# Blockwise causal attention with a gated output layer: ten transposes of the attention output go from TensorE to transposing transfers, in a new order of work

## Chip, cores and metric

One core of one Trainium2 chip runs the kernel; the seven others are idle. The metric is the device time of one execution in microseconds (us), the median of the runs given. Lower is better.

## What is computed

Two layers in a row. First attention over 8 batches and 8 heads, 576 positions of 64 features each, under a mask of blocks of 64 positions: a position sees all positions of its own block and of the blocks before it. Then a gated linear unit over the 512 features that the 8 heads make together: a causal convolution of 5 taps gives the gate, a matrix product gives the value, and their product goes through an output matrix.

```python
def _attn_ref(q, k, v):                       # [8, 8, 576, 64] each
    scores = (1.0 / np.sqrt(D)) * np.matmul(q, k.transpose(0, 1, 3, 2))
    mask = (pos[:, None] // 64) >= (pos[None, :] // 64)
    scores = np.where(mask, scores, -1000000000.0)
    attn = np.exp(scores - np.max(scores, axis=-1, keepdims=True))
    attn = attn / (np.sum(attn, axis=-1, keepdims=True) + 1e-09)
    return np.matmul(attn, v)

def _moe_ref(x, w_val, conv_w, w_out):        # x: [8, 576, 512]
    for k in range(5):
        gate_pre += conv_w[k] * xp[:, k:k + S, :]     # xp: x behind 4 rows of zeros
    gate = 1.0 / (1.0 + np.exp(-gate_pre))
    return (gate * (x @ w_val)) @ w_out
```

## The kernel before, in words

**Pieces of work.** Each batch has 4 pairs of heads, so there are 32 pairs `p` (batch `p // 4`) and 16 quads `Q` of four heads (two pairs, `2Q` and `2Q + 1`; half a batch). A quad's q and k are loaded (`Lq`, `Lk`, lines 159 to 168), cast to 16 bits (`cq`, `ck`) and turned feature-major by VectorE's stream transposes (`dq`, `dk`, line 202). TensorE makes the scores in three thirds `s.Q.0` to `s.Q.2` (line 236); ScalarE takes the exponentials `e.p.t` of one pair and third (line 244); GpSimd writes zeros over the masked corners (`m.p`, line 261). The last 64 rows of a batch have a small piece of their own (`sl.b`, `el.b`). `av.p` (line 270) multiplies by V on TensorE, with a column of ones beside V that gives the sum; `n.p` (line 286) divides by that sum on VectorE, a reciprocal and a product, and writes the pair's output `x16` in 16 bits, position-major, into one of 4 buffers.

**From position-major to feature-major.** The second layer needs features on the partitions. `xtr.p` (line 294) transposes the 128-position blocks of pairs `p` and `p + 1`, five each, on TensorE: ten transposes into two PSUM banks. `xt.p` (line 302) copies the two banks into the batch's `xts` tile in SBUF, which has room for 4 pairs of 4 + 576 + 64 columns; there are two such tiles, used by batches in turn. `xe.b` (line 305) copies the last 64 columns, with the 4 before them, to the tile of the tails.

**Second layer.** Of each batch, "token groups" `n` = 0 to 7 hold the first 512 positions and `n` = 8, 9 hold the tails of four batches each. `cn.n` (line 321) is the convolution on TensorE, 80 small matmuls with diagonal weights that read `xts` at five offsets; `th.n.s` (line 331) its tanh on ScalarE; `val.n.x` (line 336) the value's matmuls, which also read `xts`; `gv.n.x` (line 345) joins gate and value on VectorE; `o.n.t` (line 352) multiplies by the output matrix; `oc.n.t` (line 360) copies the result out of PSUM on VectorE or ScalarE; `st.n.t` (line 369) stores it.

**Order.** Nothing here is chosen by a scheduler. The string `PLAN` (line 11) lists the steps in one order, and each engine runs its own steps in the order of that list. A word is a step and, behind the `@`, its engine (`A` ScalarE, `D` VectorE, `P` GpSimd, `S` SyncE) or its PSUM banks (digits, two banks for each digit where the step takes a pair). The loop at line 450 issues them. Waits on data and on buffers come from the framework. All transfers but two go through SyncE's queue (SP), where one that waits keeps all behind it back.

Of the kernel before, what the change touches and what calls it, by code (L numbers as in the profile page):

```python
# [20 lines left out]
e.4.1@A xt.2.2@D xe.0@P wv.2@P ck.4@P wv.3@D Lv.1.3@S e.5.1@A cn.0@04 m.5@P dk.3@D dq.3@D Lv.1.2@S
Lv.1.1@S th.0.0@A val.0.0@2 cv.1.2@P gv.0.0@D Lvt.1@S val.0.1@3 th.0.1@A Lq.4@S s.3.2@06 Lwo.0@S
val.0.3@2 e.7.2@A gv.0.1@D sl.1@46 dk.4@D gv.0.3@D Lq.5@S cv.1.1@P e.6.2@A cv.1.3@D Lwo.3@S
val.0.2@3 Lvt.2@S gv.0.2@D el.1.0@A cq.4@D px.1@P pp.5@P s.3.0@04 cvt.1@P el.1.1@A e.6.0@A e.7.0@A
Lwo.1@S dq.4@D cv.1.0@P av.5@6 s.3.1@20 n.5@D m.4@P av.4@4 Lv.2.0@S cq.5@D e.7.1@A Lk.5@S e.6.1@A
m.7@P n.4@D m.6@P s.4.0@06 av.7@2 av.6@4 e.8.0@A ck.5@P n.7@D n.6@D e.9.0@A Lk.6@S s.4.1@06 e.8.1@A
# [14 lines left out]
e.17.0@A n.14@D n.15@D o.2.1@0 oc.2.1@D Lv.5.2@S s.8.2@26 Lk.10@S e.16.2@A xtr.14.2@4 xtr.12.2@0
Lk.11@S xt.14.2@D e.17.2@A cq.10@P o.2.0@2 oc.2.0@A s.8.1@46 xt.12.2@D e.16.1@A e.17.1@A cn.3@02
cq.9@P cv.4.3@D val.3.1@4 val.3.2@5 Lvt.5@S dk.9@D xe.3@P Lv.5.1@S dq.9@D th.3.0@A gv.3.1@D th.3.1@A
s.9.0@06 e.18.0@A gv.3.2@D val.3.0@4 gv.3.0@D cvt.5@D e.19.0@A o.2.2@5 Lq.11@S oc.2.2@D sl.4@02
cv.4.0@P dq.10@D o.2.3@4 el.4.0@A cvt.4@P cv.4.1@P Lv.6.3@S s.9.1@06 el.4.1@A e.18.1@A oc.2.3@D
m.16@P Lk.12@S cv.4.2@P st.1.1@S e.19.1@A ck.10@D av.16@2 n.16@D cn.8@40 val.8.0@6 th.8.1@A th.8.0@A
m.17@P s.9.2@02 e.19.2@A dk.10@D gv.8.0@D val.3.3@7 ck.12@P gv.3.3@D av.17@4 e.18.2@A Lv.5.0@S
s.10.0@26 n.17@D cq.11@A Lv.6.1@S m.19@P e.20.0@A av.19@0 st.2.0@S m.18@P av.18@4 val.8.1@2 e.21.0@A
n.19@D n.18@D s.10.1@06 e.20.1@A xtr.16.2@4 gv.8.1@D Lq.12@S e.21.1@A xtr.18.2@2 xt.16.2@D xt.18.2@D
s.10.2@04 e.20.2@A ck.11@P e.21.2@A cn.4@26 m.21@P cq.12@P dq.11@D th.4.0@A dk.11@D xe.4@P o.3.1@0  # L50
oc.3.1@D val.4.0@1 th.4.1@A s.11.0@24 m.20@P gv.4.0@D val.4.3@0 o.3.0@1 cv.5.3@A e.23.0@A cv.5.2@P
cv.5.1@D gv.4.3@D sl.5@46 e.22.0@A val.4.1@0 el.5.0@A el.5.1@A s.11.1@24 cv.5.0@D val.4.2@6 Lvt.6@S
dq.12@D oc.3.0@A gv.4.1@D gv.4.2@D e.22.1@A o.3.3@7 Lk.14@S dk.12@D ck.14@P st.2.1@S e.23.1@A
oc.3.3@A Lk.13@S s.11.2@02 av.20@4 e.22.2@A Lk.15@S n.20@D av.21@6 o.4.0@0 e.23.2@A oc.4.0@A
s.12.0@24 e.24.0@A e.25.0@A n.21@D xtr.20.2@6 Lv.7.3@S Lq.13@S Lv.6.0@S m.22@P cq.13@A xt.20.2@D
m.23@P av.23@0 st.3.0@S av.22@2 n.23@D s.12.1@46 e.25.1@A Lv.7.1@S o.3.2@0 n.22@D oc.3.2@D
xtr.22.2@2 xt.22.2@D Lv.6.2@S ck.13@P e.24.1@A cv.6.3@D o.4.1@1 cv.6.1@A Lv.7.0@S oc.4.1@A Lq.14@S
s.12.2@46 cn.5@20 dk.13@D xe.5@P e.25.2@A m.25@P dq.13@D e.24.2@A o.4.3@6 oc.4.3@D o.4.2@7 cv.6.0@D
th.5.1@A th.5.0@A oc.4.2@D sl.6@04 el.6.1@A o.8.1@6 Lv.7.2@S el.6.0@A s.13.2@02 Lq.15@S Lvt.7@S
cvt.7@D val.5.0@7 dk.14@D cq.14@P oc.8.1@D e.27.2@A dq.14@D e.26.2@A val.5.1@4 gv.5.0@D s.13.0@25  # L60
e.27.0@A val.5.3@0 e.26.0@A gv.5.1@D val.5.2@1 s.13.1@46 cq.15@P st.3.1@S e.27.1@A e.26.1@A cvt.6@D
o.8.0@2 m.24@P cv.6.2@D gv.5.3@D gv.5.2@D o.5.0@3 ck.15@D m.26@P cv.7.1@P s.14.0@06 oc.8.0@A
oc.5.0@A av.25@4 e.29.0@A av.26@2 dq.15@D dk.15@D e.28.0@A av.24@6 n.25@D s.14.1@04 e.29.1@A m.27@P
# [6 lines left out]
o.6.0@4 o.6.3@5 xt.30.2@A oc.6.3@A cn.7@26 oc.6.1@A th.7.1@A xe.7@P th.7.0@A oc.6.2@D val.7.1@0  # L70
gv.7.1@D val.9.0@1 val.7.3@5 cn.9@26 th.9.0@A gv.9.0@D val.9.1@0 th.9.1@A val.7.2@2 gv.9.1@D
oc.6.0@A val.7.0@1 gv.7.2@D o.9.0@0 o.9.1@4 gv.7.0@D st.6.1@S gv.7.3@D oc.9.1@A st.6.0@S o.7.0@1
oc.9.0@D o.7.1@0 o.7.2@2 oc.7.0@A o.7.3@1 oc.7.1@D st.9.0@S st.7.0@S oc.7.2@D oc.7.3@AD st.7.1@SA
# [411 lines left out]
```

## Time and profile before

| | |
|---|---|
| median of 3 runs | 176.98 us (176.69 to 178.0) |
| the profiled execution | 176.23 us |
| its span, from first to last instruction | 174.4 us, so 1.8 us lie around it |
| mean granted TensorE clock | 0.971 |
| busy: TensorE matmul (PE) | 161.7 us, 93% |
| busy: TensorE weight load (PEld) | 94.8 us, 54% |
| busy: VectorE (DVE) | 129.9 us, 74% |
| busy: ScalarE (ACT) | 131.5 us, 75% |
| busy: GpSimd (POOL) | 69.2 us, 40% |
| moved by DMA | 40.30 MB, 231 GB/s over the span |

A line of a group gives the source line, the engine and its operation, what is written and read, the shape and the count; then the busy time and the mean length of one; then how long the engine was idle before these instructions and what ended that. A line of the timeline starts with the start and the length in us and ends with a count. The matmuls of the profile overlap, so what a step costs TensorE is read from its start to the next step's start, not from its length.

### The profile page before, as it was taken

The numbers are of one execution on the slowest core, as the hardware profiler recorded it, in microseconds if no ns is written. First come the engines' busy times: TensorE is split into PE (matmuls) and PEld (weight loads), VectorE is DVE, ScalarE is ACT, GpSimd is POOL, SyncE is SP. The second block draws the span as 40 slices with busy tenths as digits, with TensorE's granted clock in tenths as the row PEclk, the third lists the DMA queues.
The fourth block names the chain that finished last, engine by engine and source line by source line (L and its number), as shares of the span: only waits on it lengthen the run. The fifth ranks groups of instructions, "written<-read, shape, count | busy, mean of one in ns | idle before, by whom it ended". The sixth has DMA issues, their size and how long they took to land.

```text
span 174.4 us, 6916 instructions
## 1 busy us (share of the span) xinstructions
PE 161.7 (93%) x3013; PEld 94.8 (54%) x3013; DVE 129.9 (74%) x202; ACT 131.5 (75%) x160; POOL 69.2 (40%) x141
## 2 busy tenths in 40 slices
PE   7448999989999999999999999999999999999990
PEld 2123677367445673576366854675437563855640
DVE  1599399998878887879697798779899836741650
ACT  3039999987969899767979799899879698456320
POOL 1284565954595817085505134433603022210000
PEclk9985599999999999999999999999999999999999
DMA  5999997999799699999997596999320005403246
GB/s 176 397 323 296 381 327 195 312 264 301 194 336 271 187 325 334 277 296 319 343 337 242 114 402 198 305 233 357 136 79 2 4 4 194 172 4 120 81 163 241
DMA packets 48216, 40.30 MB, mean 231 GB/s; under 512 B 38453, under 2 KB 38453, under 8 KB 48186
## 3 DMA queue, kind: packets, MB, share of 16 engines
q1 hardware_dynamic: 47898, 39.01, 72.8%
q10 hardware_dynamic: 288, 0.85, 1.4%
q8 instruction: 23, 0.38, 0.9%
q14 instruction: 7, 0.06, 0.1%
HBM read 30.42 MB, written 9.44 MB: 228 GB/s over the span
## 4 chain that ended last, share of the span: by engine, by line
PE 70%; DVE 12%; ACT 7%; issue 5%; DMA 3%; ACTq 0%; DVEq 0%
PE PS L99 65%; ACT pt L242 6%; PE PS L298 5%; DMA qks<-in_q_dram 3%; DVE x L290 3%; DVE qk L156 2%; DVE kT L202 2%; DVE gv L347 2%; DVE qT L202 1%; DVE osb L156 1%; DVE rc L289 1%; ACT osb L156 1%; DVE xt L156 0%; DVE v16t L156 0%; ACT v L156 0%
## 5 line engine op out<-in xcount | busy, mean ns | idle before, releaser
L242 ACT ACTIVATE pt<-PS 128x1024 f16<-128x1024 f32 (+1 forms) x112 | 97.8, 937 | 23.3 <-PE PS L99 20.9
L99 PE MATMUL PS<-qT,kT 32*128 32x64 f16 (+4 forms) x768 | 37.6, 291 | 5.7 <-DVE kT L202 4.5
L99 PEld LDWEIGHTS <-pt 128*128 128x128 f16 x960 | 32.0, 99 | 7.1 <-issue 3.1
L99 PE MATMUL PS<-w_out,gv 128*128 128x512 f16 x144 | 35.3, 380 | 0.1
L347 DVE SCALAR_TENSOR_TENSOR gv<-th,PS 128x512 f16<-128x512 f32 x36 | 24.0, 681 | 14.6 <-ACT th L332 9.3
L156 POOL CAST qk<-qks 128x1152 f16<-128x1152 f32 x22 | 25.3, 1165 | 21.4 <-DVE kT L202 12.3
L99 PE MATMUL PS<-v,pt 128*128 128x65 f16 x896 | 33.0, 195 | 0.9 <-ACT pt L242 0.7
L99 PE MATMUL PS<-xt,w_val 128*128 128x512 f16 x128 | 31.9, 381 | 0.0
L99 PEld LDWEIGHTS <-kT 32*128 32x128 f16 x768 | 16.2, 95 | 28.2 <-issue 16.7
L263 POOL MEMSET pt<- 64x384 f16 x32 | 13.8, 430 | 37.8 <-ACT pt L242 37.1
L290 DVE TENSOR_TENSOR x<-PS,rc 128x640 f16<-128x640 f32 x32 | 26.4, 824 | 1.1
L99 PEld LDWEIGHTS <-w_val 128*128 128x128 f16 x160 | 13.7, 98 | 14.6 <-issue 3.8
L99 PEld LDWEIGHTS <-gv 128*128 128x128 f16 x144 | 12.8, 98 | 14.4 <-issue 0.9
L202 DVE STREAM_TRANSPOSE qT<-qk 128x576 f32<-128x576 f32 x16 | 19.9, 1243 | 0.1
L202 DVE STREAM_TRANSPOSE kT<-qk 128x576 f32<-128x576 f32 x16 | 19.7, 1243 | 0.0
L332 ACT ACTIVATE th<-PS 128x1024 f32<-128x1024 f32 (+1 forms) x20 | 17.7, 947 | 2.2 <-PE PS L99 2.2
L156 DVE COPY osb<-PS 128x512 f32<-128x512 f32 (+1 forms) x20 | 13.4, 671 | 7.3 <-PE PS L99 5.8
L156 ACT COPY osb<-PS 128x512 f32<-128x512 f32 (+1 forms) x17 | 9.7, 583 | 9.0 <-PE PS L99 8.3
L289 DVE RECIPROCAL rc<-PS 128x10 f32<-128x10 f32 x32 | 6.8, 212 | 8.4 <-PE PS L99 5.7
L156 DVE COPY xt<-PS 128x1152 f16<-128x1152 f16 x14 | 10.2, 754 | 3.8 <-PE PS L298 3.7
L156 POOL COPY xtl<-xt 128x272 f16<-128x272 f16 x7 | 3.9, 551 | 22.0 <-DVE xt L156 16.7
L156 POOL CAST v<-vst 128x512 f16<-128x512 f32 x18 | 11.4, 642 | 3.0 <-DMA vst<-in_v_dram 2.4
(45 smaller groups left out, 113.8 us busy)
## 6 DMA issues: line engine op xcount, KB each, us to landing
qks<-in_q_dram SPq DMA_DIRECT2D x16, 576.0 KB, 7.0
qks<-in_k_dram SPq DMA_DIRECT2D x15, 576.0 KB, 7.0
vst<-in_v_dram SPq DMA_DIRECT2D x32, 256.0 KB, 6.4
out_dram<-osb SPq DMA_DIRECT2D x15, 512.0 KB, 4.3
out_dram<-osb SPq DMA_DIRECT2D x5, 256.0 KB, 2.5
vtst<-in_v_dram SPq DMA_DIRECT2D x8, 128.0 KB, 5.4
th<-in_moe_w_val_dram SPq DMA_DIRECT2D x2, 512.0 KB, 8.9
w_st<-in_moe_w_out_dram SPq DMA_DIRECT2D x4, 256.0 KB, 8.7
```

The lines of the kernel that those rows point to most:

```text
L99: nc.tensor.matmul(out=out, lhsT=lhsT, rhs=rhs, start=start, stop=stop, skip_group_check=True)
L156: (eng.copy if eng is nc.scalar else eng.tensor_copy)(out=o, in_=i)
L202: m.transpose(out=o.bitcast(fp32)[..., 0], in_=qk16[(2 * Q + i) % NQ16][0:128].bitcast(fp32))
L242: nc.scalar.activation(out=o, in_=i, func=AF.Exp, bias=0.0, scale=0.125)
L263: m.memset(pt[64:128, 0:2, 0:1536].rearrange("p h (t s) -> p h t s", t=3)[:, :, :, 0:64], 0.0)
L289: nc.vector.reciprocal(out=rc, in_=O[:, :, :, 64:65])
L290: nc.vector.tensor_tensor(out=x16[p % NX16][0:128].rearrange("p i h d -> p h i d"), in0=O[:, :, :, 0:64], in1=rc.to_broadcast([128, 2, 5, ...
L298: nc.tensor.transpose(out=f16(bk(m, e))[:, 128 * i:128 * i + 128], in_=x16[(p + e) % NX16][0:128, i, 0:2, 0:64], identity=ident16[0:128, 0 ...
L332: nc.scalar.activation(out=ths[turn(n) % NTH][0:128, 2 * s:2 * s + 2, 0:width(n)], in_=two(slot["cn", n][s])[:, :, 0:width(n)], func=AF.Ta ...
L347: nc.vector.scalar_tensor_tensor(out=gvs[turn(n) % NGV][0:128, e * x:e * x + e, 0:w], in0=ths[turn(n) % NTH][0:128, e * x:e * x + e, 0:w], ...
```

## The change

- `xtr` and `xt` of pairs 20, 22, 24, 26 and 28 (quads 10 to 14, batches 5 and 6 and half of batch 7) are gone: 50 TensorE transposes, four copies on VectorE and one on ScalarE.
- In their place stand ten steps `xd.p`, p = 20 to 29, on SyncE's queue: each is one transposing transfer of one pair, from `x16` (128 positions by 5 x 128) straight into `xts` (128 features by 5 x 128). Quads 0 to 9 and quad 15 stay on TensorE.
- `xts` is laid out 16 + 576 + 64 columns wide instead of 4 + 576 + 64, and the readers are shifted by 12 columns.
- The order of the list is kept up to the scores of quad 7 (`s.7.0`), with other PSUM banks in places, and is a new one from there to the end. In the new one some steps change engine (`xt.12` and `ck.14` go to ScalarE, `xt.30` to VectorE, some casts and copies likewise), and the last copy of the program, `oc.7.3`, is one instruction on ScalarE and no longer two halves on ScalarE and VectorE.

```diff
-    xts = ring(NX, [128, 4, 644], fp16, "xt")
+    xts = ring(NX, [128, 4, 656], fp16, "xt")
...
     def evac_x(p, cnt, m):
-        copy(m, xts[(p // 4) % NX][0:128, p % 4:p % 4 + 2, 4:580], f16(two(slot["xtr", p]))[:, :, 0:576])
+        copy(m, xts[(p // 4) % NX][0:128, p % 4:p % 4 + 2, 16:592], f16(two(slot["xtr", p]))[:, :, 0:576])
+
+    def dma_x(p, m):
+        m.dma_start_transpose(out=xts[(p // 4) % NX][0:128, p % 4, 16:656].rearrange("p (i s) -> p i s", s=128),
+                              in_=x16[p % NX16][0:128].rearrange("p i h d -> p (i h d)"))
...
-        copy(m, xtl[b // 4][0:128, 0:4, pr, 0:68, o], xts[b % NX][0:128, 0:4, 512:580])
+        copy(m, xtl[b // 4][0:128, 0:4, pr, 0:68, o], xts[b % NX][0:128, 0:4, 524:592])
...
-            return xts[n % NX][r, g, kk:kk + 512]
+            return xts[n % NX][r, g, 12 + kk:524 + kk]
...
-        m.memset(xts[i][0:128, 0:4, 0:4], 0.0)
+        m.memset(xts[i][0:128, 0:4, 12:16], 0.0)
...
-        "xe": ends_x, "cn": conv, "th": gate, "val": val, "gv": gated, "o": proj, "oc": evac_out, "st": store, "cwc": cast_taps, "cw": taps,
+        "xe": ends_x, "xd": dma_x, "cn": conv, "th": gate, "val": val, "gv": gated, "o": proj, "oc": evac_out, "st": store, "cwc": cast_taps, "cw": taps,
```

Of the list itself, the stretch that turns batch 6 (quads 12 and 13) and holds its convolution `cn.6`, with what stood there before:

```diff
-o.5.3@0 cv.7.3@D s.15.1@24 xtr.26.2@6 xt.26.2@D oc.5.3@A e.30.1@A xtr.24.2@0 s.14.2@26 xt.24.2@D
-xe.6@P e.31.1@A e.29.2@A m.29@P cn.6@04 o.5.2@6 e.28.2@A val.6.0@7 m.28@P cv.7.0@P th.6.0@A oc.5.2@D
...
+cvt.7@P av.27@2 s.14.1@04 cv.7.0@P e.28.1@A n.24@D n.27@D o.5.2@6 oc.5.2@D e.29.1@A s.15.1@20
+e.30.1@A o.5.3@7 xd.26@S o.5.1@6 e.31.1@A xd.24@S oc.5.1@A xd.27@S s.14.2@24 oc.5.3@D e.29.2@A
+Lv.7.2@S cn.6@06 m.29@P val.6.3@4 e.28.2@A m.28@P val.6.1@5 th.6.1@A cv.7.1@D gv.6.3@D th.6.0@A
```

**TensorE ahead of `cn.6`.** `qT`, `kT` are the turned queries and keys of one quad, `x` the pairs' outputs (buffers 0 to 3), `DG` the diagonal weights of the convolution. Before:

```order
L99 MATMUL PS<-qT_92,kT_95 128x64
...
L298 MATMUL PS<-ident_63,x_2_115 128x128
...
L298 MATMUL PS<-ident_63,x_1_114 128x128
...
L99 MATMUL PS<-qT_94,kT_97 128x320
...
L99 MATMUL PS<-xt_117,DG 32x512
```

Now:

```order
L99 MATMUL PS<-qT_92,kT_95 128x64
...
L99 MATMUL PS<-w_out,gv_123 128x512
...
L99 MATMUL PS<-qT_94,kT_97 128x320
...
L99 MATMUL PS<-xt_117,DG 32x512
```

The twenty transposes between `s.15.1` and `s.14.2` are gone, and two output products (`o.5.3`, `o.5.1`) stand there instead; `cn.6` still follows `s.14.2`.

**SyncE's queue around the transfers of batch 5.** `vst` are the staging buffers of V, `osb` those of the output. Now:

```order
L161 DMA qks_76<-in_q_dram 128x1152
L306 DMA_TRANSPOSE xt_118<-x_0_113 128x5x128
L306 DMA_TRANSPOSE xt_118<-x_1_114 128x5x128
L306 DMA_TRANSPOSE xt_118<-x_3_116 128x5x128
L306 DMA_TRANSPOSE xt_118<-x_2_115 128x5x128
L171 DMA vst_85<-in_v_dram 128x8x64
L176 DMA vtst_87<-in_v_dram 64x8x64
L171 DMA vst_78<-in_v_dram 128x8x64
L171 DMA vst_82<-in_v_dram 128x8x64
```

Before, the last loads stood in a row:

```order
L171 DMA vst_82<-in_v_dram 128x8x64
L161 DMA qks_76<-in_q_dram 128x1152
L171 DMA vst_84<-in_v_dram 128x8x64
L161 DMA qks_72<-in_q_dram 128x1152
L176 DMA vtst_87<-in_v_dram 64x8x64
L378 DMA out_dram<-osb_129 128x2x512
```

The transposing transfers of batch 5 stand behind the last load of q; four loads of V (`Lv.7.3`, `Lvt.7`, `Lv.6.0`, `Lv.7.0`) now stand behind them. Those of batch 6 have one load of V behind them (`Lv.7.2`), those of pairs 28 and 29 stores alone.

**VectorE around batch 6.** `rc` and `x` are the two halves of `n`. Before:

```order
L156 COPY osb_129<-PS 128x512
L289 RECIPROCAL rc_110<-PS 128x10
L290 TENSOR_TENSOR x_3_116<-PS,rc_110 128x2x5x64
L156 CAST v_1_99<-vst_85 128x8x64
L156 COPY xt_117<-PS 128x2x576 x2
L156 COPY osb_126<-PS 128x512
```

Now:

```order
L289 RECIPROCAL rc_110<-PS 128x10
L290 TENSOR_TENSOR x_3_116<-PS,rc_110 128x2x5x64
L156 COPY osb_126<-PS 128x512 x2
L156 CAST v_1_99<-vst_83 128x8x64
L351 SCALAR_TENSOR_TENSOR gv_124<-th_122,PS 128x512
```

The two copies of `xt` behind the norms are gone; nothing of VectorE's lies between a norm and the convolution's data any more.

More of the change, by code (lines that the diff above doesn't have):

```diff
@@ L21 @@
[L21 to L26, printed above, removed]
@@ L29 @@
+m.7@P n.4@D m.6@P s.4.0@60 av.7@4 av.6@2 e.8.0@A ck.5@P n.7@D n.6@D e.9.0@A Lk.6@S s.4.1@06 e.8.1@A
+Lwo.2@S Lv.2.2@S wo.1@P xtr.4.2@4 Lv.2.3@S Lq.6@S xt.4.2@D wo.0@P e.9.1@A xtr.6.2@2 s.4.2@04 e.8.2@A
+xt.6.2@D e.9.2@A m.9@P dq.5@D Lv.2.1@S cn.1@26 val.1.0@0 th.1.0@A dk.5@D xe.1@P gv.1.0@D Lq.7@S
 ck.6@P val.1.1@1 s.5.0@24 cq.6@P th.1.1@A e.11.0@A e.10.0@A gv.1.1@D o.0.1@0 oc.0.1@D o.0.2@1
@@ L41 @@
[L41 to L63, printed above, removed]
@@ L70 @@
[L70 to L73, printed above, removed]
+m.13@P th.2.0@A o.1.3@2 oc.1.3@D m.12@P dq.8@D o.1.0@3 sl.3@06 val.2.2@2 th.2.1@A el.3.1@A gv.2.2@D
+ck.8@P s.7.0@46 el.3.0@A cv.3.1@A cv.3.2@D e.15.0@A oc.1.0@A o.1.2@0 Lq.9@S oc.1.2@D val.2.3@1
@@ new lines @@
+Lq.10@S e.14.0@A Lk.9@S s.7.2@26 Lv.4.1@S dk.8@D e.15.2@A Lv.4.0@S val.2.1@0 gv.2.3@D av.12@4
+gv.2.1@D e.14.2@A s.7.1@60 e.15.1@A val.2.0@2 n.12@D Lvt.4@S cq.9@P gv.2.0@D av.13@4 e.14.1@A
+cv.4.1@A s.8.0@02 m.15@P o.2.0@6 n.13@D e.17.0@A av.15@4 m.14@P oc.2.0@D e.16.0@A s.8.2@26 e.16.2@A
+Lk.10@S av.14@0 n.15@D o.2.1@4 ck.9@P n.14@D e.17.2@A oc.2.1@A xtr.12.2@2 xt.12.2@A xtr.14.2@0
+s.8.1@46 xt.14.2@D dk.9@D e.16.1@A cn.3@02 dq.9@D e.17.1@A th.3.1@A Lv.4.2@S cv.4.2@D st.0.1@S
+cvt.4@P val.3.2@4 m.16@P m.17@P th.3.0@A val.3.1@5 s.9.0@26 Lv.4.3@S Lv.5.3@S o.2.3@0 cv.4.0@A
@@ new lines @@
+cv.7.3@P gv.6.0@D s.15.2@02 e.31.2@A m.31@P e.30.2@A m.30@P av.29@6 av.28@4 n.29@D n.28@D av.31@2
+av.30@0 o.6.2@4 n.31@D o.6.0@5 oc.6.2@A st.8.0@S n.30@D xtr.30.2@0 xd.29@S o.6.3@4 xt.30.2@D o.6.1@2
+xd.28@S oc.6.0@D oc.6.3@A cn.7@06 val.7.0@3 th.7.0@A st.5.0@S xe.7@D oc.6.1@D th.7.1@A val.9.0@2
+st.6.0@S cn.9@04 th.9.1@A gv.7.0@D th.9.0@A gv.9.0@D val.7.1@3 val.9.1@4 gv.9.1@D val.7.2@5 gv.7.2@D
+val.7.3@2 o.9.0@4 o.9.1@5 gv.7.3@D gv.7.1@D o.7.0@0 o.7.1@1 o.7.3@2 o.7.2@3 oc.9.1@A oc.7.0@A
+oc.9.0@D oc.7.1@D st.6.1@S st.9.0@S oc.7.2@A st.7.0@S oc.7.3@A st.7.1@SA
```

47 lines of the change are left out of this document (31 added, 16 removed).

## Prediction

> **What bounds the kernel now.** I read the page's busy times first, then a table of windows, then TensorE's timeline.
>
> ```profile
> span 174.4 us, 6916 instructions
> PE 161.7 (93%) x3013; PEld 94.8 (54%) x3013; DVE 129.9 (74%) x202; ACT 131.5 (75%) x160; POOL 69.2 (40%) x141
> ```
>
> The windows give, after the length, the busy time of PE, PEld, DVE, ACT and POOL, the granted clock, the DMA share and GB/s. The first shown begins where the new order does (`s.7.0`).
>
> ```profile
> 67.60:97.00 29.40, 29.38 (x615) 17.84 (x615) 23.36 (x38) 24.09 (x30) 13.18 (x24) 1.00 0.97 294
> 97.00:117.00 20.00, 19.93 (x394) 12.18 (x390) 16.32 (x25) 17.68 (x22) 6.84 (x13) 1.00 0.88 263
> 117.00:142.00 25.00, 24.86 (x438) 13.94 (x431) 22.47 (x34) 21.18 (x28) 5.87 (x12) 1.00 0.32 109
> 142.00:170.20 28.20, 28.15 (x496) 16.26 (x495) 14.08 (x24) 15.64 (x19) 3.83 (x11) 1.00 0.31 115
> ```
>
> In none of these windows is TensorE idle for more than 0.14 us, and its clock is full: it alone is the bound from 67.6 us to the last matmul, and a step taken from it is worth its whole time. VectorE (22.5 of 25.0) and ScalarE (21.2) come close between 117 and 142. The DMA share falls from 0.97 to 0.32: late in the kernel there is room for transfers.
>
> **The steps removed.** The five `xtr` that go, as a group of the stretch 113.5 to 153.3 us (busy us, mean ns of one):
>
> ```profile
> L298 PE MATMUL PS<-ident,x 128*128 128x128 f16 x50 | 3.5, 219 | 0.0
> ```
>
> Matmuls overlap, so what a step costs is read in TensorE's timeline from its start to the next step's start:
>
> ```profile
> 114.01 0.73 PE L298 MATMUL PS<-ident,x 128*128 128x128 f16 x10
> 114.58 0.90 PE L99 MATMUL PS<-v,pt 128*128 128x65 f16 x24
> ...
> 139.76 1.29 PE L298 MATMUL PS<-ident,x 128*128 128x128 f16 x20
> 141.00 0.96 PE L99 MATMUL PS<-qT,kT 32*128 32x320 f16 x16
> 142.00 1.35 PE L99 MATMUL PS<-xt,DG 32*32 32x512 f16 x80
> ...
> 147.51 0.63 PE L99 MATMUL PS<-qT,kT 32*128 32x320 f16 x16
> 148.07 0.91 PE L99 MATMUL PS<-v,pt 128*128 128x65 f16 x24
> ...
> 149.00 0.89 PE L99 MATMUL PS<-v,pt 128*128 128x65 f16 x24
> ...
> 164.81 5.34 PE L99 MATMUL PS<-w_out,gv 128*128 128x512 f16 x24
> ```
>
> `xtr.20` is 114.58 - 114.01 = 0.57, `xtr.26` and `xtr.24` together are 141.00 - 139.76 = 1.24, and `xtr.22` and `xtr.28`, the same ten transposes each, I count like the first: 0.57 + 1.24 + 2 x 0.57 = **2.95 us**, below the group's 3.5, as it must be.
>
> A small wait behind them goes too. `s.14.2` takes 142.00 - 141.00 = 1.00, where the same third of quad 15 takes 148.07 - 147.51 = 0.56: half of its banks were those of `xtr.26` and not yet copied out by `xt`. That is **0.44 us**.
>
> **The copies removed.** Four of VectorE's `xt`, 0.75 us each by the groups below, and one of ScalarE's. Neither engine is the bound, so I count nothing; `xt.12`, moved to ScalarE, costs nothing while `cn.3` waits for `xt.14` on VectorE anyway. If VectorE were the bound, they would be worth 3.0 us more; if `cn.3` had no other wait, `xt.12` would cost the 0.4 us by which ScalarE is the slower.
>
> ```profile
> L347 DVE SCALAR_TENSOR_TENSOR gv<-th,PS 128x512 f16<-128x512 f32 x36 | 24.0, 681 | 14.6 <-ACT th L332 9.3 <-PE PS L99 2.9 <-ACT pt L242 2.1
> ...
> L202 DVE STREAM_TRANSPOSE kT<-qk 128x576 f32<-128x576 f32 x16 | 19.7, 1243 | 0.0
> ...
> L156 DVE COPY xt<-PS 128x1152 f16<-128x1152 f16 x14 | 10.2, 754 | 3.8 <-PE PS L298 3.7
> ...
> L156 ACT COPY osb<-PS 128x512 f32<-128x512 f32 x16 | 9.3, 596 | 6.9 <-PE PS L99 6.2 <-ACT pt L242 0.6
> ...
> L156 ACT COPY xt<-PS 128x1152 f16<-128x1152 f16 x2 | 2.2, 1120 | 3.5 <-PE PS L298 3.5
> ```
>
> **The transfers added.** TensorE no longer turns the data itself; it waits for it at `cn.5`, `cn.6` and `cn.7`. What matters is the last transfer of each batch: from the end of its `av`, through the norm, to the convolution. The norm first:
>
> ```profile
> 138.35 0.82 DVE L290 TENSOR_TENSOR x<-PS,rc 128x640 f16<-128x640 f32 x1
> 139.09 0.42 DVE L156 CAST v<-vst 128x512 f16<-128x512 f32 x1
> ...
> 149.27 0.22 DVE L289 RECIPROCAL rc<-PS 128x10 f32<-128x10 f32 x1 [0.83 <-ACT pt L242]
> 149.53 0.82 DVE L290 TENSOR_TENSOR x<-PS,rc 128x640 f16<-128x640 f32 x1
> ```
>
> `av.28` begins at 148.07 and gives way on TensorE at 149.00; its norm ends at 149.53 + 0.82 = 150.35, 1.35 us later. The work that TensorE has in between, in the new order, from the rows above (a third of scores 0.56; an `o` 5.34 / 6 = 0.89; an `av` 149.00 - 148.07 = 0.93):
>
> - `cn.5`: behind `av.22` stand `s.12.1`, `o.4.3`, `o.3.2`, `s.12.2`, `o.4.1`, `o.4.2`: 2 x 0.56 + 4 x 0.89 = 4.7, less 1.35 leaves **3.3 us**.
> - `cn.6`: behind `av.27` stand `s.14.1`, `o.5.2`, `s.15.1`, `o.5.3`, `o.5.1`, `s.14.2`: 3 x 0.56 + 3 x 0.89 = 4.35, which leaves **3.0 us**.
> - `cn.7`: behind `av.28` stand `av.31`, `av.30`, four `o` and `xtr.30`: 2 x 0.93 + 4 x 0.89 + 0.57 = 6.0, which leaves **4.6 us**.
>
> So the transfers cost TensorE nothing if the last of them takes up to 3 us from the end of its norm to its landing. The trace of before has no transposing transfer; the nearest rows are (KB, median us to landing):
>
> ```profile
> vst<-in_v_dram SPq DMA_DIRECT2D x32, 256.0 KB, 6.4
> out_dram<-osb SPq DMA_DIRECT2D x15, 512.0 KB, 4.3
> out_dram<-osb SPq DMA_DIRECT2D x5, 256.0 KB, 2.5
> ```
>
> One `xd` moves 128 x 640 x 2 bytes = 160 KB, less than any of them. The 6.4 belongs to loads of V that queue at a DMA share near 1; stores of 256 KB, most of them late on idle engines, land in 2.5. At the 294 GB/s of the first window 160 KB are 0.56 us of moving, less than the 1 us at which the norms deliver them. Bounds: **2.5 below, 6.4 above**. I take 2.5, the row that it is nearest to: from 117 us on the engines are two thirds idle, and the list puts the last loads of q and k ahead. That is **0 us** of stall. With 4.3 the stalls are 1.0 + 1.3 + 0 = 2.3 us; with 6.4 they are 3.1 + 3.4 + 1.8 = 8.3 us.
>
> SP stands at each `xd` until its norm is done, and four loads of V queue behind those of batch 5. The first to be needed, `Lv.6.0`, is used by `av.25`, and ahead of that TensorE has the rest of the 3.3 us, `cn.5` (1.3 like the row at 142.00), four `val` of batch 5 (four matmuls of the size of an `o`'s), three `o` and three thirds of scores: about 12 us against 6.4 and a cast. `Lv.7.2`, behind batch 6, is used by `av.29`, over 5 us after `cn.6` begins. I count 0; if that cover were gone, TensorE would wait at `av.25` for just as long as V is late.
>
> **The new order.** I followed banks and exponentials through it with the starts above. Four places wait a little: `cn.6` for ScalarE's copy `oc.5.1` (0.3, inside the transfer's slack), `av.16` for an exponential, `s.13.1` and `s.15.1` for their banks (0.1 each): **+0.6 us**. From `cn.4` to `cn.5` (19.7 us of TensorE's work) VectorE gets seven turns of q and k, four norms, four `gv`, four `oc` of the same size and three smaller steps: 7 x 1.24 + 4 x 1.04 + 8 x 0.68 + 1.9 = 20.2 us by mean lengths. Neighbours overlap, though: in the norm's rows the cast starts at 139.09, while the product ends at 138.35 + 0.82 = 139.17. At 0.08 us less for each of 26 instructions it is 18.1 us, so VectorE just follows. From both sides: 0 to 1.5 us for the order as a whole; I keep 0.6.
>
> **The end.** The last copy was two halves, one after the other:
>
> ```profile
> 170.23 0.37 ACT L156 COPY osb<-PS 128x256 f32<-128x256 f32 x1 [2.05 <-PE PS L99]
> 170.64 0.42 DVE L156 COPY osb<-PS 128x256 f32<-128x256 f32 x1 [0.62 <-ACT osb L156]
> ```
>
> From 170.23 to 171.06 is 0.83; ScalarE's whole copy takes 0.60 by its group. **-0.2 us**.
>
> **The sum**: -2.95 - 0.44 + 0.6 - 0.2 = **-3.0 us**. The profiled execution, 176.23 with a span of 174.4 and 1.8 around it, would become 173.2; the median of the runs stands 0.75 higher, so I predict 176.98 - 3.0 = **174.0 us**. Its own range is 172.9 (none of the small waits, and half a microsecond more from the order) to 175.2.
>
> **Rivals.**
>
> 1. *The transfers land late and TensorE waits at the three convolutions.* For it: no trace shows such a transfer, and half of the loads of V need 6.4 or more. Against: those are waits in a full queue. At 4.3 us it gives 174.0 + 2.3 = 176.3, within 1%; from about 4.7 the stalls eat the gain, and at the upper bound it is 174.0 + 8.3 = **182.3, slower**. If they even ran strictly one behind the other at 6.4 each, four in a row would end 25.6 us after the first can start, some 3 us before the last norm ends: waits of 25.6 - 3 - 3.3 = 19 at `cn.5`, 19 at `cn.6` and, with two in a row, 12.8 - 1 - 4.6 = 7 at `cn.7`, together about 219.
>
> The Trainium skill ("VectorE: DVE Perf Modes", section "The three transpose paths") speaks for this rival: it gives 1309 ns to a 128 x 128 transpose by DMA against 390 ns on TensorE, and advises TensorE where a PSUM destination will do. My estimate from that page is 5 x 1.309 = 6.5 us for one `xd` if its five blocks follow each other; no row here shows whether they do. On TensorE's side this trace disagrees with the page: ten such transposes take 0.57 us.
>
> 2. *The bound passes to VectorE or ScalarE.* The new order packs the same exponentials and turns into 3 us less, and VectorE had 22.5 of 25.0 before. If turns and `gv` come late by the 1.5 us of my upper bound (0.9 more than I count) and exponentials by another 1 us, it is 174.0 + 1.9 = **175.9**, within 1%. Against: four copies left VectorE in the same stretch.
>
> **Chances.** Forecast 0.62; rival 1 in its mild form (about 4 us) 0.10, in its hard form (over 5.5 us) 0.18; rival 2 0.10. A measurement tells about 1% (1.8 us) from no change. So faster by over 1% (under 175.2): 0.62; within 1%: 0.20; slower: 0.18. The range reaches from 172.9 to 180.0, which leaves out the worst half of rival 1 and a little below.
>
> **What would show it.** PE's busy time falls to about 158 us, with no idle time of over 0.3 us ahead of the convolutions (`xt,DG`), and the row of `xt<-x` lands in 2.5 to 3 us. Landing over 4 us, and PE idle before `xt,DG` released by DMA, is rival 1. PE idle behind VectorE's `gv`, `qT`, `kT` or ScalarE's `pt` is rival 2. A span that falls by less than 2.5 us with neither shows that I mis-sized the removed steps: the transposes' time would then have come back as longer `av` or `o`.

## The result, and the profile after

| | before | after |
|---|---|---|
| median of 14 runs each, same chip | 176.72 us | 178.44 us |
| ratio | | 1.0077, interval 1.0047 to 1.0106 |
| the profiled execution | 176.23 us | 178.01 us |
| from the first instruction to `s.7.0` | 67.66 us | 69.69 us |
| from `s.7.0` to the end of the last matmul | 102.49 us | 102.18 us |
| behind the last matmul, to the span's end | 4.28 us | 4.36 us |

The ratio is not that of the two medians: it compares the runs as a whole, without one of after (180.7 us) that fell in a slower state of the chip. The changed kernel is 0.8% slower; the forecast was 1.7% faster. The stretch that was reordered did become shorter, by 0.31 us, and the stretch that was not reordered became 2.03 us longer. The page's first rows after:

```profile
span 176.2 us, 6837 instructions
PE 160.2 (91%) x2963; PEld 92.7 (53%) x2963; DVE 127.4 (72%) x196; ACT 130.7 (74%) x161; POOL 70.1 (40%) x140
```

The 50 transposes are gone (3013 matmuls have become 2963), but PE's share has fallen from 93 to 91%: TensorE now stands still. The windows, cut as in the prediction, show where (length, then PE, PEld, DVE, ACT, POOL, clock, DMA share, GB/s):

```profile
69.70:97.00 27.30, 26.43 (x542) 15.86 (x541) 21.25 (x33) 25.30 (x32) 8.42 (x17) 1.00 0.99 302
97.00:117.00 20.00, 19.56 (x371) 11.73 (x372) 16.44 (x24) 16.54 (x21) 8.73 (x17) 1.00 0.75 224
117.00:142.00 25.00, 24.42 (x463) 13.82 (x459) 19.91 (x30) 19.65 (x25) 10.10 (x19) 1.00 0.74 151
142.00:171.90 29.90, 29.81 (x512) 16.52 (x506) 15.74 (x29) 15.58 (x20) 2.84 (x9) 1.00 0.49 157
```

TensorE is idle for 27.30 - 26.43 = 0.87 us in the first of them, where no transfer of the change runs yet, and for 0.58 us in the third, with `cn.5`. Three places explain most of it.

**Ahead of `s.7.0`: a bank.** TensorE's timeline at the first `av`, before and then after:

```profile
16.66 2.01 PE L99 MATMUL PS<-qT,kT 32*128 32x320 f16 x18
18.68 1.48 PE L99 MATMUL PS<-v,pt 128*128 128x65 f16 x24
```

```profile
16.64 2.23 PE L99 MATMUL PS<-qT,kT 32*128 32x320 f16 x22
20.07 1.48 PE L99 MATMUL PS<-v,pt 128*128 128x65 f16 x24 [1.21 <-POOL pt L435]
```

`av.1` starts 1.39 us later. The profile names a zeroing of GpSimd's, done at 18.79 us; what ends the wait is ScalarE's exponential `e.3.0`:

```profile
18.90 2.85 ACT L242 ACTIVATE pt<-PS 128x1024 f16<-128x1024 f32 x3 [0.17 <-PE PS L99]
```

It is the first of these three, about 0.95 us long, and reads bank 0, into which `av.1` now wants to write (`av.1@0` behind `s.1.0@40`; before it was `av.1@4` behind `s.1.0@60`). Behind it TensorE runs at half clock for longer, in windows of 2 us before and after:

```profile
20.00:22.00 2.00, 1.99 (x35) 1.45 (x33) 1.38 (x3) 1.83 (x3) 0.00 (x0) 0.61 1.18 377
22.00:24.00 2.00, 1.72 (x45) 1.18 (x42) 1.96 (x4) 2.00 (x3) 0.84 (x3) 1.00 1.02 389
```

```profile
20.00:22.00 2.00, 1.93 (x34) 1.81 (x38) 0.01 (x1) 1.76 (x2) 0.02 (x1) 0.50 1.17 373
22.00:24.00 2.00, 2.00 (x39) 1.51 (x32) 1.97 (x3) 1.11 (x2) 0.00 (x0) 0.50 1.01 405
```

The granted clock stays at 0.50 until 25.23 us where before it was back at 1.00 at 21.58. By `val.0.0` (29.84 us before, 32.20 after) the lag has grown from 1.39 to 2.36 us; 0.33 of it is won back by `s.7.0`. What of this the clock alone cost, and what small waits did, is not separated. Nor is the longer slow stretch (13.65 us, against 10.24 before) a sign of the wait by itself: the traces of experiments 9, 10 and 12, with before's banks and no wait at `av.1`, have 13.65 too. What goes with the banks is its end: 25.2 to 26.3 us in the three traces with the new banks (after, experiments 2 and 4), 20.4 to 23.3 in the twelve with the old.

**`cn.5`: the fourth transfer.** SP's timeline, the landing (median, us) and VectorE's last norm ahead of it; then TensorE:

```profile
116.98 6.14 SPq L306 DMA_TRANSPOSE xt<-x  x4
...
137.03 6.31 SPq L306 DMA_TRANSPOSE xt<-x  x4
...
153.21 2.56 SPq L306 DMA_TRANSPOSE xt<-x  x2
```

```profile
xt<-x SPq DMA_TRANSPOSE x10, 2.8
```

```profile
119.65 0.82 DVE L290 TENSOR_TENSOR x<-PS,rc 128x640 f16<-128x640 f32 x1
```

```profile
123.87 0.39 PE L99 MATMUL PS<-xt,DG 32*32 32x512 f16 x2
124.83 1.34 PE L99 MATMUL PS<-xt,DG 32*32 32x512 f16 x78 [0.57 <-DMA xt<-x]
```

Four issues fill 6.14 us of SP: single ones took 1.32, 1.92, 1.22 and 1.23 us. (Why the second took 1.92 is not shown; at 1.22 the fourth would have gone out some 0.7 us earlier, by an estimate from these rows.) The norms arrive one per us (119.65 - 118.66 for the last two), so the queue falls behind. The last norm ends at 119.65 + 0.82 = 120.47, its issue begins at 121.89 and its data are there at 124.78: the landing itself is 2.9 us, the wait for SP another 1.4. `cn.5` loses 0.95 us (0.15 before), `cn.6` 0.28.

**`av.17`: no wait at all.** Inside its 24 matmuls TensorE stops, and the profile says "issue", that is, nothing it shows released it:

```profile
94.92 1.04 PE L99 MATMUL PS<-xt,w_val 128*128 128x512 f16 x4
95.79 0.74 PE L99 MATMUL PS<-v,pt 128*128 128x65 f16 x19
97.42 0.32 PE L99 MATMUL PS<-v,pt 128*128 128x65 f16 x5 [0.89 <-issue]
```

Between the start of these 19 and the next 5 lie 1.63 us, where nineteen take some 0.55: 1.08 us are lost, and the whole step takes 1.06 us more than before. The only queue that brings something for TensorE without a semaphore is the page's queue of instructions:

```profile
q8 instruction: 23, 0.38, 0.9%
```

Its 23 transfers are of 16,384 bytes, and the last instruction ahead of TensorE's stop is number 3259 (matmuls and weight loads counted together, from 0) = 13 x 256 - 69, in the middle of a step. Both traces have 23 such transfers and 23 places 256 k - 69, and nearly every transfer starts just as TensorE passes such a place, or up to 7 us later. The one wanted at 3259 started 1.17 us after TensorE had passed the place ahead of it in before, and 2.86 us in after.

The account, by starts of steps (us): 2.03 ahead of `s.7.0`; -2.93 for the five `xtr`, as long as they were in before's trace; -0.43 at `s.14.2`, whose wait is gone; +1.08 at `cn.5` and `cn.6`; +1.06 at `av.17`; +0.08 at the end. The spans differ by 1.80, which leaves +0.91 for all other steps of the new order, the largest 0.36 at `s.8.1`.

### The profile page after: what moved, and what is told of

Same layout as the page of the kernel before. It is cut to its first block, busy times and chain, and to the rows that moved or that the text cites. A ratio compares the mean times of both kernels' runs of the same rounds, so it can differ in the third digit from the quotient of the medians.

```text
span 176.2 us, 6837 instructions
## 1 busy us (share of the span) xinstructions
PE 160.2 (91%) x2963; PEld 92.7 (53%) x2963; DVE 127.4 (72%) x196; ACT 130.7 (74%) x161; POOL 70.1 (40%) x140
## 4 chain that ended last, share of the span: by engine, by line
PE 65%; ACT 11%; DVE 9%; issue 5%; DMA 5%; POOL 3%; POOLq 0%; ACTq 0%; DVEq 0%
PE PS L99 62%; ACT pt L242 7%; DVE x L290 3%; PE PS L298 3%; DMA qks<-in_q_dram 3%; DMA xt<-x 2%; DVE qk L156 1%; ACT osb L156 1%; POOL qk L156 1%; ACT th L336 1%; DVE qT L202 1%; DVE rc L289 1%; DVE xt L156 1%; DVE kT L202 1%; POOL pt L263 1%
## 5 line engine op out<-in xcount | busy, mean ns | idle before, releaser
L99 PEld LDWEIGHTS <-pt 128*128 128x128 f16 x960 | 32.9, 100 | 9.8 <-issue 3.6
L99 PE MATMUL PS<-v,pt 128*128 128x65 f16 x896 | 34.3, 197 | 2.9 <-POOL pt L435 1.2
L156 POOL CAST qk<-qks 128x1152 f16<-128x1152 f32 x23 | 26.8, 1178 | 11.4 <-DMA qks<-in_k_dram 6.6
L99 PEld LDWEIGHTS <-kT 32*128 32x128 f16 x768 | 15.7, 95 | 27.0 <-issue 16.1
L156 DVE COPY osb<-PS 128x512 f32<-128x512 f32 x20 | 13.7, 687 | 7.3 <-PE PS L99 6.9
L156 ACT COPY osb<-PS 128x512 f32<-128x512 f32 x16 | 9.4, 592 | 11.9 <-PE PS L99 11.9
L99 PE MATMUL PS<-xt,DG 32*32 32x512 f16 x640 | 11.6, 377 | 1.3 <-DVE xt L156 0.8
L99 PEld LDWEIGHTS <-DG 32*32 32x32 f16 x800 | 9.5, 88 | 5.1 <-issue 2.4
L156 POOL CAST v<-vst 128x512 f16<-128x512 f32 x17 | 10.6, 630 | 3.9 <-DMA vst<-in_v_dram 3.6
```

The source lines that it names most:

```text
L99: nc.tensor.matmul(out=out, lhsT=lhsT, rhs=rhs, start=start, stop=stop, skip_group_check=True)
L156: (eng.copy if eng is nc.scalar else eng.tensor_copy)(out=o, in_=i)
```

## The experiments

Each ratio is against before, from runs on the same chip.

**1 and 2: the banks.** Two kernels swap only the PSUM banks of 27 early steps. The first puts before's banks into the changed kernel, the second the changed ones into before. Of the edit the first six steps, without what stands between them:

```diff
-sl.0@46 s.1.2@26 s.1.0@40 av.1@0 s.1.1@46 av.0@2
+sl.0@64 s.1.2@24 s.1.0@60 av.1@4 s.1.1@06 av.0@4
```

> The changed kernel with the PSUM banks of the kernel before in the 27 early steps (up to sl.3) where they differ, nothing else. Theory (bank): av.1 in banks 0 and 1 waits for the exponential e.3.0 that still reads bank 0, where banks 4 and 5 were free; the pause at half clock also holds the low clock for one 3.4 us window more. Then s.7.0 starts near 67.7 us and no longer at 69.7, the low clock lasts 10.2 us and no longer 13.7, and the time falls by about 2.0 us, to 0.997 of the kernel before or a little less. Rival (chance of the early loads, or of the clock): s.7.0 stays near 69.7 in the profile and the time stays at 1.008.

> The kernel before with the early PSUM banks of the changed kernel, nothing else changed. Theory (bank): it carries the whole early loss, s.7.0 starts near 69.7 us, and it takes 1.009 to 1.013 of the kernel before (+1.6 to +2.2 us). Rival (chance, or something in the new order): no difference, 1.000.

Measured: 0.9963 (0.9927 to 0.9999) for before's banks in the changed kernel, against 1.0077 without them; 1.0098 (1.0056 to 1.014) for the new banks in before, +1.7 us. The second kernel's TensorE shows the same wait at the same place:

```profile
20.28 1.48 PE L94 MATMUL PS<-v,pt 128*128 128x65 f16 x24 [1.21 <-POOL pt L426]
```

So the early banks alone turn a small gain into a loss. It follows too that transfers and late order together gain 0.4%, not the forecast 1.7. One expectation failed: with the banks put back `s.7.0` started at 68.8 us, not near 67.7. The wait at `av.1` was gone (0.01 us), but TensorE stood 1.07 us inside `xtr.6`, with nothing to release it, a stop like that in `av.17`; experiments 5 to 7 come back to it.

**3: more work ahead of `cn.5`.** From here on, except in experiment 4, before's banks stay in. Two steps that wait for nothing new move ahead of `cn.5`:

```diff
-o.4.2@2 dk.14@D oc.4.2@D dk.13@D cn.5@64
+o.4.2@2 o.8.1@3 dk.14@D oc.4.2@D oc.8.1@D dk.13@D cn.5@64
```

> As the run with the early banks restored, and the output product o.8.1 with its copy is moved ahead of the convolution cn.5 (bank 3 for bank 0), which gives the transfers of batch 5 0.9 us more cover. Theory (SyncE needs 1.2 us or more to issue each transposing transfer, so that the fourth leaves 1.4 us after its norm): cn.5 waits under 0.2 us in place of 0.95, and the time falls by about 0.9 us against the run with the banks alone. Rival (the transfers hold up other work, or the wait is passed on): cn.5 begins later but s.13.2 or val.5 waits instead, and the time is that of the run with the banks alone.

Measured: 0.9968 (0.9933 to 1.0002), the same as without the move.

```profile
124.36 1.35 PE L94 MATMUL PS<-xt,DG 32*32 32x512 f16 x80
...
127.48 0.30 PE L94 MATMUL PS<-qT,kT 32*128 32x64 f16 x16
128.55 0.64 PE L94 MATMUL PS<-qT,kT 32*128 32x320 f16 x16 [0.78 <-ACT pt L237]
```

All 80 matmuls of `cn.5` run in one piece, and 4 us later `s.13.2` waits 0.78 us for an exponential. The wait was passed on: ScalarE is now the late one. `av.17` stopped here too, for 1.43 us.

**4: a smaller transfer.** In the changed kernel, with its own banks, each transfer takes four of the five blocks (the last 64 positions of batches 5 and 6 and of half of batch 7 are left out).

```diff
-        m.dma_start_transpose(out=xts[(p // 4) % NX][0:128, p % 4, 16:656].rearrange("p (i s) -> p i s", s=128),
-                              in_=x16[p % NX16][0:128].rearrange("p i h d -> p (i h d)"))
+        m.dma_start_transpose(out=xts[(p // 4) % NX][0:128, p % 4, 16:528].rearrange("p (i s) -> p i s", s=128),
+                              in_=x16[p % NX16][0:128, 0:4].rearrange("p i h d -> p (i h d)"))
```

> The changed kernel with transposing transfers of four of the five blocks of each pair; the last block (positions 512 to 575 of batches 5, 6 and half of 7) is left out, so that part of the output is not computed. If the issue on SyncE costs by the amount moved, an issue falls from 1.2 to about 1.0 us and the two long ones (1.9 and 2.1) by more, and cn.5 waits 0.3 to 0.8 us less. If it is a fixed cost of an issue, it stays at 1.2 us.

Measured, in one run: 179.21 us, and

```profile
118.48 6.05 SPq L306 DMA_TRANSPOSE xt<-x  x4
```

```profile
xt<-x SPq DMA_TRANSPOSE x10, 2.7
```

A fifth less data leaves four issues at 6.05 us (6.14 with five blocks), the landing at 2.7 and the wait of `cn.5` at 0.95. Between these two sizes issue and landing are nearly a fixed price per transfer, not one by amount.

**5, 6 and 7: the stop in `av.17`.** On top of experiment 3, the fifth kernel puts 80 tiny matmuls into TensorE's idle time at the start, which moves every later instruction by 160 places; the sixth moves one `val` ahead of the wait of `s.13.2`; the seventh does both.

```diff
-w.512@0 s.0.2@02 s.0.1@46
+w.512@0 w.64@0 w.64@0 w.64@0 w.64@0
...
-sl.6@24 Lv.7.0@S el.6.1@A gv.5.0@D st.4.0@S el.6.0@A s.13.2@46 e.27.2@A e.26.2@A val.5.2@1 val.5.1@0
+sl.6@24 val.5.1@0 Lv.7.0@S el.6.1@A gv.5.0@D st.4.0@S el.6.0@A s.13.2@46 e.27.2@A e.26.2@A val.5.2@1
```

> Kernel: the one with before's banks in the early part and the two steps o.8.1, oc.8.1 moved ahead of cn.5 (ratio 0.9968 to before, TensorE stands still for 1.43 us inside av.17 there), plus 80 tiny matmuls of 64 columns on the warm-up bank, put into TensorE's idle time at the start. They change no result; they only move every later instruction by 160 places in TensorE's program, so that its 16 KB pieces begin elsewhere. Theory 1 (instruction fetch: TensorE arrives at a piece that the full DMA queues have not brought yet): the gap inside av.17 is gone or below 0.3 us, no gap of the same kind over 0.5 us elsewhere, and the time falls by about 1.4 us against that kernel, ratio to before about 0.989. Theory 2 (the gap belongs to av.17 itself, its banks or its data): the gap stays inside av.17 at 1 us or more and the ratio stays at about 0.997. If the tiny matmuls disturb the clock at the start, s.7.0 starts later than 69.0 us; then the gap alone decides.

> The same kernel without the tiny matmuls, with val.5.1 moved between sl.6 and s.13.2. There the wait of cn.5 for its data had gone, and s.13.2 then stood 0.78 us for ScalarE's exponential el.6. Theory (a step of 0.9 us put ahead of the wait is done in it): the wait of s.13.2 falls to about 0, no step up to cn.6 takes it over, and the time falls by 0.8 us: ratio about 0.992. Rival (it is passed on once more, since ScalarE is the late one and val.5.1 only shifts who shows it): waits of together 0.5 us or more appear between s.13.2 and s.14.0, and the ratio stays at about 0.997.

> Both edits together: tiny matmuls at the start and val.5.1 ahead of s.13.2. If the fetch gap (1.4 us) and the wait of s.13.2 (0.8 us) are two separate losses, both go: 2.2 us less than the kernel with neither, ratio to before about 0.985. If one is only the other's shadow (a stall that gives ScalarE the time it lacks), the gain is that of the larger one alone, ratio about 0.989 to 0.992.

Measured: 1.0071 (1.0028 to 1.0114), 0.9971 (0.9922 to 1.0021) and 1.0048 (1.0007 to 1.0089). In the fifth kernel `av.17` runs through, and `s.9.0`, nine us earlier, is cut in two:

```profile
86.66 0.39 PE L99 MATMUL PS<-qT,kT 32*128 32x512 f16 x1
88.32 0.63 PE L99 MATMUL PS<-qT,kT 32*128 32x512 f16 x7 [1.26 <-issue]
```

The stop followed the count of instructions, not the step: now it lies at 3003 = 12 x 256 - 69. That tells against any cause in `av.17` itself. But the time I had hoped for did not come, since the new places had no more room. The largest of the further stops is in `cn.1`, at 1467 = 6 x 256 - 69:

```profile
44.59 0.63 PE L99 MATMUL PS<-xt,DG 32*32 32x512 f16 x25
46.27 1.06 PE L99 MATMUL PS<-xt,DG 32*32 32x512 f16 x55 [1.04 <-issue]
```

Two smaller ones, of 0.4 and 0.5 us, came at `o.2.1` and `cn.4`, and the seventh kernel too stands in `av.7` (1.07 us) and `cn.1` (1.62). What decides is how long before TensorE reaches the next such place its piece has landed (us, from the starts and lengths of these transfers in the traces):

```
kernel            stop at   transfer starts  takes   landed ahead   TensorE
                            behind 256k-69           of TensorE     stands
before            -         1.17             0.96     2.13          0
after             av.17     2.86             0.97     0.25          1.08
experiment 3      av.17     3.16             0.99    -0.07          1.43
experiment 4      av.17     3.52             1.34    -0.78          1.75
experiment 5      s.9.0     5.60             0.96    -0.24          1.66
experiment 7      s.9.0     4.92             1.72    -0.53          1.32
experiment 12     -         1.27             0.96     2.04          0
```

The same holds for all 332 places 256 k - 69 (from k = 2) in the 15 traces of the study. Where the piece landed less than 0.5 us ahead of TensorE, or behind it, TensorE stood, 15 times out of 15, for 0.9 to 2.4 us; where it landed over 1.1 us ahead, TensorE stood for more than 0.4 us not once in 310; the seven between stood for up to 0.5 us. At `av.17` this happened in all five traces that have the new order and the count of after, and in none of the eight with before's order. But a stop is not tied to the order alone: at `xtr.6`, which both orders have, four traces with before's banks stood for over a microsecond and before itself did not.

The start is late where the other queues are full: in the new order the DMA share stays at 1 from 84 to 102 us, in before it falls to 0.40 at 94 and 0.20 at 96 us. That full queues cause the late start is read from these traces; a kernel with the loads alone thinned out was not tried. Moving `val.5.1` gained nothing that could be measured (the sixth against the third). In the seventh kernel's trace the wait of `s.13.2` is gone and `o.8.0` waits 0.29 us: the step filled the wait, but that it saves time isn't shown.

**8: the transposes alone, order of before.** `xd` in the places of `xtr`, all else as before.

```diff
-e.25.0@A n.21@D xtr.20.2@6 Lv.7.3@S Lq.13@S Lv.6.0@S
+e.25.0@A n.21@D xd.20@S xd.21@S Lv.7.3@S Lq.13@S Lv.6.0@S
```

> The transposes alone: before's order and before's banks throughout, with the ten transposing transfers in the places where xtr and xt of quads 10 to 14 stood. Theory (issue and landing decide: 1.2 to 2 us per issue on SP, 2.8 us to land; TensorE saves 2.95 us of transposes and the 0.44 us of s.14.2): there is too little work between the last av of a batch and its convolution, so TensorE waits about 2.6 us at cn.5, 3.1 us at cn.6 and about 0 at cn.7, and the time is about 2.2 us longer than before, ratio about 1.012. Rival (the new order itself costs what the transfers gained, the transfers do not): waits below 1 us at both convolutions and a ratio of about 0.985.

Measured: 1.0959 (1.0888 to 1.1031), +17 us where 2.2 were expected. SP's timeline, and behind it ScalarE's and TensorE's:

```profile
99.78 1.35 SPq L156 DMA_DIRECT2D qks<-in_k_dram  x1
114.56 2.64 SPq L301 DMA_TRANSPOSE xt<-x  x2
117.30 1.30 SPq L166 DMA_DIRECT2D vst<-in_v_dram  x1
118.65 0.56 SPq L156 DMA_DIRECT2D qks<-in_q_dram  x1
```

```profile
123.97 1.15 ACT L151 CAST qk<-qks 128x1152 f16<-128x1152 f32 x1 [6.28 <-DMA qks<-in_q_dram]
```

```profile
127.01 1.04 PE L94 MATMUL PS<-qT,kT 32*128 32x320 f16 x16 [6.72 <-ACT pt L237]
```

From 101 to 114 us SP issues nothing: it stands at `xd.20`, whose norm isn't done, and `Lq.13` behind it goes out at 118.65, where before it went at 105.64. ScalarE waits 6.28 us to cast it, and the exponentials behind the cast keep `s.12.2` back by 6.72. The long waits of this kernel also went with a lower clock: the granted clock is 0.50 from 124.5 to 131.3 us and from 155.2 to 162.1.

**9 to 11: fewer transfers, and loads ahead.** The tenth kernel puts the transfers of batch 5 behind the load of quad 14's q. The ninth and eleventh use only six transfers, those of the quad of each batch that comes first, and leave the others on TensorE. In the ninth `xtr.26` also writes a bank that `oc.5.3` had yet to read, so one tile of batch 5's output is overwritten there.

```diff
-Lv.7.0@S oc.4.1@A Lq.14@S s.12.2@46 cn.5@20
+Lv.7.0@S oc.4.1@A Lq.14@S xd.20@S xd.21@S xd.23@S xd.22@S s.12.2@46 cn.5@20
```

and in the eleventh

```diff
+Lv.7.0@S oc.4.1@A xd.20@S xd.21@S Lq.14@S s.12.2@46 cn.5@20
```

> Before's order and banks, but only the quad of each of batches 5, 6 and 7 that comes first (pairs 20 and 21, 24 and 25, 28 and 29) goes by transposing transfers, six in all; the other quad of the batch stays on TensorE. The first two stand on SP behind the load of q of quad 14 and ahead of the last three loads. xtr.26 takes the bank that xtr.24 had, so that s.14.2 finds its banks free. Theory (a transfer costs SP 1.2 us and lands 2.8 us after it was issued; with over 4 us of TensorE's work behind its norm, and no needed load behind it on SP, it is hidden): 3 x 0.57 us of transposes and up to 0.44 us at s.14.2 go, no wait at cn.5, cn.6 or cn.7 for xt over 0.2 us, and the time falls by 1.7 to 2.1 us: ratio about 0.989. Rival (transfers cost elsewhere, in loads that come late behind them or in other transfers' time): ratio 1.00 or above, with waits at s.13, s.14 or av.25 of together 1.5 us or more.

> The transposes alone once more: before's order with all ten transfers, but those of batch 5 stand on SP behind the load of q of quad 14 (issued at 113 us in before) and no longer ahead of Lv.7.3, Lq.13 and the others. Theory (the 17 us that the first such kernel lost were loads held on SP behind a transfer that waits for its norm; issue and landing alone cost about what was expected): SP issues loads between 100 and 114 us again, the 6.8 us at o.4.1 and s.12.2 and the 3.2 us at s.13.0 are gone, and there stay waits of about 2 us at cn.5 and 2 to 3 us around cn.6 against 3.4 us saved: ratio 1.005 to 1.015. Rival (the transfers themselves take that much from TensorE or from the loads): the ratio stays above 1.04.

> As the kernel with six transfers, with two things put right: xtr.26 keeps its bank of before (in the other kernel it took bank 0 ahead of the copy oc.5.3 that still had to read it, and TensorE stood 3.1 us there), and the first two transfers stand ahead of the load of q of quad 14 on SP. Theory (a transfer with over 4 us of TensorE's work behind its norm and no early-needed load behind it is hidden): 3 x 0.57 us of transposes go, the waits at cn.5 (0.4 us there) and at xtr.26 are gone, av.30 waits 0.4 us for its exponentials; 1.3 us less than before, ratio about 0.993. Rival (in before's order the time that TensorE saves is waited for ScalarE or VectorE at the next step): waits at s.14, cn.6 and av.30 of together 1.5 us or more, ratio 1.00 or above.

Measured: 1.0181 (1.0108 to 1.0254), 1.0402 (1.032 to 1.0483) and 1.0244 (1.0172 to 1.0315). The loads ahead brought back 10 of the 17 us, less than expected, and six transfers still lost. ScalarE in the eleventh kernel says why:

```profile
138.80 0.66 ACT L237 ACTIVATE pt<-PS 128x256 f16<-128x256 f32 x2 [0.40 <-PE PS L94]
141.98 0.59 ACT L151 COPY osb<-PS 128x512 f32<-128x512 f32 x1 [2.52 <-DMA out_dram<-osb]
```

```profile
140.21 0.73 PE L293 MATMUL PS<-ident,x 128*128 128x128 f16 x10
143.54 1.03 PE L94 MATMUL PS<-qT,kT 32*128 32x320 f16 x16 [2.60 <-ACT pt L237]
```

A copy out of PSUM waits 2.52 us for a store to give its output buffer back. The stores `st.4.0` and `st.4.1`, whose data were ready, stood on SP behind `xd.25`, which waited for its norm. With the copy, ScalarE's exponentials are late, and `s.14.2` waits 2.6 us for them; from then on the granted clock is 0.50 for 3.41 us, as in experiments 9 and 10 with their waits at `s.14.2` and `cn.6`. So it was not the bank of `xtr.26` that had held the ninth kernel up there, as I had thought: with the bank put right the wait stayed.

**12 and 13: stores ahead too.** In six-transfer and ten-transfer form:

```diff
+st.4.0@S st.4.1@S
 n.25@D
+xd.25@S
...
+st.5.0@S st.8.0@S
 n.28@D
+xd.28@S
```

> As the last kernel with six transfers (ratio 1.0244), but the stores st.4.0 and st.4.1 stand on SP ahead of the transfers of batch 6, st.5.0 and st.8.0 ahead of those of batch 7, and the load Lvt.7 ahead of those of batch 5. Theory (held queue: there ScalarE's copy oc.5.3 waited 2.52 us for the landing of a store that stood behind a transfer waiting for its norm, its exponentials came late, and s.14.2 waited 2.6 us, after which the clock fell): that wait, the 1.0 us inside cn.6 and the 0.7 us at s.13.0 are gone, 3 x 0.57 us of transposes stay saved, and the ratio is 0.990 to 0.996. Rival (ScalarE sets the pace from s.13 to s.15.1, and the time of the transposes had been its cover): s.14.2 and its neighbours wait for exponentials by 1.2 us or more in place of the transposes, ratio 1.000 or above.

> The transposes alone a third time: before's order, all ten transfers, loads and stores that held things up put ahead of them as in the other kernel of this call. Theory (what is then left is the transfers' own cost: issue spacing 1.2 to 2 us and 2.8 us of landing against too little work of TensorE in between): waits of about 1.6 us at cn.5 and 2.3 us around cn.6, none over 0.6 us elsewhere, less 3.4 us saved: ratio 1.002 to 1.008. Rival (the held queue was not what cost the 7 us of the second such kernel): waits at s.13.0, s.15.1, s.14.2 stay at 1.2 us or more each, ratio above 1.025.

Measured: **0.9936 (0.9903 to 0.9969)** with six transfers, the fastest kernel of the study, 1.1 us below before; 1.0085 (1.0046 to 1.0125) with ten. The whole step from 1.0244 to 0.9936 is the place of four stores and one load in SP's queue; what each of the five is worth was not tried. What is left in the ten-transfer kernel:

```profile
120.92 1.34 PE L93 MATMUL PS<-xt,DG 32*32 32x512 f16 x78 [0.97 <-DMA xt<-x]
```

```profile
141.72 0.64 PE L93 MATMUL PS<-qT,kT 32*128 32x320 f16 x16 [1.18 <-ACT pt L236]
```

`cn.5` waits 0.97 us for its last transfer, less than the 1.6 expected. At batch 6 `s.14.2` waits 1.18 us for an exponential, in the place where twenty transposes of 1.24 us had stood, so only the 0.43 of `s.14.2`'s own wait is gained there, and `cn.6` loses another 0.8 us. The six-transfer kernel at batch 6:

```profile
139.53 0.73 PE L292 MATMUL PS<-ident,x 128*128 128x128 f16 x10
140.78 0.96 PE L93 MATMUL PS<-qT,kT 32*128 32x320 f16 x16 [0.52 <-ACT pt L236]
141.67 1.36 PE L93 MATMUL PS<-xt,DG 32*32 32x512 f16 x80
```

From the transposes to `cn.6` it takes 2.14 us; before, with twenty transposes instead of ten, it took 142.00 - 139.76 = 2.24. Here the removed ten were worth 0.1 us, not 0.57: `s.14.2` cannot begin before ScalarE has read its bank, and the transposes had stood in that wait. From `s.7.0` on this trace is 0.65 us shorter than before's: 0.24 up to `cn.5`, 0.31 from there to `s.15.1`, 0.10 here, and nothing at batch 7, where `av.30` and `o.6.2` take 0.43 and 0.13 us longer in place of the 0.56 of `xtr.28`.

## Why the prediction was wrong, point by point

- **"With other PSUM banks in places": no term of the sum stood for it.** This step failed and alone decides the sign. I followed banks through the new part of the list only and took the part whose order is kept as unchanged. It was put at nothing and cost 2.03 us in the trace; the two bank experiments give 1.7 and 2.0.
- **"Less than the 1 us at which the norms deliver them".** This failed next. I had priced the moving (0.56 us), not SP's issue, which took 1.2 to 2.1 us. The last transfer of batch 5 so landed 4.3 us behind its norm, against 3.3 of cover: 1.08 us at `cn.5` and `cn.6`. Counted from the issue, the landing was 2.8, right within the size of the row that gave 2.5; counted from the norm's end, as the sum needs it, the 2.5 should have been 4.3. Rival 1 named the right place with the wrong mechanism: a slow landing; it was a queue of issues. So my sign for it, a landing of over 4 us, did not show.
- **The estimate from the Trainium skill** ("VectorE: DVE Perf Modes", section "The three transpose paths") of 5 x 1309 ns = 6.5 us for one transfer: this trace disagrees. Five blocks landed 2.8 us behind the issue and four in 2.7, so blocks don't follow each other at that price. The 0.57 us that the prediction sets against 390 ns on TensorE are ten transposes in a row; the record of a single one is 219 ns long in before's trace.
- **"I count 0" for SP's holding.** Right for the change, whose order has its loads and stores in places that suit: neither `av.25` nor `av.29` waits in its trace. As a price it was far off: in before's order the same ten transfers cost 17 us, 15.5 of which came back when loads and stores were put ahead.
- **The removed steps:** -2.95 forecast; the five steps are gone and took 2.93 in before's trace, and of the 0.44 at `s.14.2` 0.43 came. That each transpose is worth its whole time holds where TensorE sets the pace; experiment 12 shows a place where ScalarE does, and PE's busy time fell to 160.2, not to 158.
- **The new order, +0.6:** +0.91 without `av.17`, by difference. The 1.06 us there, a stop for instructions, stood in no rival.
- **The end, -0.2:** +0.08. The last two copies are now both on ScalarE, one behind the other, so the whole copy saved nothing over two halves on two engines:

```profile
171.95 1.07 ACT L156 COPY osb<-PS 128x512 f32<-128x512 f32 x2 [2.05 <-PE PS L99]
```

- **Rival 2, ScalarE as the bound:** not what the change met, but what limits the repair: experiments 3, 12 and 13 each ended in a wait for an exponential (0.78, 0.52 and 1.18 us).
